# Attention with an off-by-one softmax, then a max-out feed-forward layer: the first two batches in a new order

## The chip, the cores and the metric

The kernel runs on one core of one Trainium2 chip. The metric is device time in microseconds (us) of one execution. Before the change the median of three runs is 368.01 us (367.05 to 368.43). The execution that the profiler recorded took 374.09 us by the same clock, and its span from the first to the last instruction is 372.2 us; all times of single instructions below are from that span.

Five engines work side by side, each on its own list of instructions in order: PE (TensorE, matrix products), DVE (VectorE), ACT (ScalarE), POOL (GpSimd, which here issues the loads) and SP (which here issues stores and crossbar transposes). They wait for one another only through semaphores.

## The reference

```python
# q, k, v: [8 batches, 12 heads, 448 positions, 64], float32
scores = q @ k.T / sqrt(64)
m = max(scores, axis=-1)
e = exp(scores - m)
attn = e / (sum(e, axis=-1) + exp(-m) + 1e-9)        # "softmax off by one"
x = (attn @ v) with the 12 heads side by side        # [3584 tokens, 768]
h = maximum(maximum(x @ w1, x @ w2), x @ w3)         # each w: [768, 768]
out = h @ w_out                                      # [3584, 768] float32
```

Without the maximum, which the kernel leaves out because it cancels, attn = exp(s) / (sum exp(s) + 1).

## The kernel before

The work is cut into 24 **groups**: batch b (8 of them) times g (3), each with four heads. A group needs k and q transposed (head dimension on the partitions), then scores, exponentials, the denominator, and the product with v. Loads by POOL turn float32 into fp16 on the way, except k and q of group 0, which SP and ACT load as float32 into tiles of their own.

**From a loaded tile to the transposed one.** DVE first copies each of k and q so that two heads lie side by side (`copy_qk`); then either PE transposes seven 128x128 blocks for each into PSUM and DVE copies that back (`pe_transpose`), or one crossbar DMA from the SP queue does both (`dma_transpose`). Groups 0 to 6 (`PE_TR = 7`) go over PE, the others over the crossbar.

```python
    def copy_qk(i, n):
        st = state.setdefault(i, {})
        if n == 0:
            st["qk16"] = p16_pool.tile([128, 2, NJ, 2, D], MMDT, tag="qk16", name="qk16")
        src = first["kq"[n]] if i == 0 else raw[i]["kq"[n]]
        nc.vector.tensor_copy(
            out=st["qk16"][:, n], in_=src.rearrange("p s j d -> p j s d")
        )
...
    def pe_transpose(i, n):
        st = state[i]
        if n == 0:
            st["qkT"] = att_pool.tile([128, 2, NJ, 128], MMDT, tag="qkT", name="qkT")
        trT = ps1.tile([128, NJ, 128], MMDT, tag="bank1", name="trT")
        for j in range(NJ):
            nc.tensor.transpose(
                out=trT[:, j, :], in_=st["qk16"][:, n, j].rearrange("p s d -> p (s d)"),
                identity=ident16,
            )
        nc.vector.tensor_copy(
            out=st["qkT"][:, n].rearrange("p j c -> p (j c)"),
            in_=trT.rearrange("p j c -> p (j c)"),
        )
        if n == 1:
            st.pop("qk16")

    def pe_transpose_both(i):
        for n in range(2):
            pe_transpose(i, n)

    def dma_transpose(i):
        st = state[i]
        st["qkT"] = att_pool.tile([128, 2, NJ, 128], MMDT, tag="qkT", name="qkT")
        nc.sync.dma_start_transpose(
            out=st["qkT"].rearrange("p n j c -> p (n j) c"),
            in_=st.pop("qk16").rearrange("p n j s d -> p (n j s d)"),
        )
```

**Scores** fill PSUM tiles of the pool `ps2` (three buffers), and ACT empties them with the exponential. The first batch is cut into two parts of positions (`PARTS`: 192 and 256 columns) so that feed-forward can start before attention of the batch is complete; from group 3 on a group is visited whole, in the units 0 to 2, 3 to 4, and 5 to 6.

```python
    PARTS = ((0, 3), (3, NJ))

    def scores_part(i, part):
        st = state[i]
        q0, q1 = PARTS[part]
        nq = (q1 - q0) * KC
        eT = e_pool.tile([128, NJ, 2, nq], MMDT, tag="eT", name="eTp")
        st["eT", part] = eT
        for j0 in range(0, NJ, 2):
            n = min(2, NJ - j0)
            stp = ps2.tile([128, 2, 512], FP32, tag="bank2", name="stp")
            for jj in range(n):
                score_tile(st["qkT"], stp[:, :, ts(jj, nq)], j0 + jj, q0, q1)
            nc.scalar.activation(
                out=eT[:, j0 : j0 + n].rearrange("p j r q -> p r j q"),
                in_=stp[:, :, 0 : n * nq].rearrange("p r (j q) -> p r j q", j=n),
                func=AF.Exp,
                scale=scale,
                bias=e_b,
            )

    def scores_visit(i, units):
        st = state[i]
        if "eT" not in st:
            st["eT"] = e_pool.tile([128, NJ, 2, S], MMDT, tag="eT", name="eT")
        stps = []
        for j in units:
            stp = ps2.tile([128, 2, 512], FP32, tag="bank2", name="stp")
            score_tile(st["qkT"], stp[:, :, 0:S], j, 0, NJ)
            stps.append((j, stp))
        for j, stp in stps:
            nc.scalar.activation(
                out=st["eT"][:, j], in_=stp[:, :, 0:S], func=AF.Exp, scale=scale, bias=e_b
            )
```

`av_part(i, part)` (letter A below) makes 28 matmuls with ones for the denominator, then on ACT a logarithm (`lnd`) and an exponential (`rb`) for its inverse, 28 matmuls with v, and on DVE the product into `xT`. For whole groups `sum_e`, `den_group` and `av_group` do this.

**Feed-forward** is a queue of `pieces`, each a run of PE matmuls that ends in one DVE operation; `moe(cols)` puts in as many as the credit allows, and after each piece one waiting DVE or SP job from `jobs`. `up_part` pieces are 12 matmuls of 192 or 256 columns (first batch), `up_piece` six of 448, `out_piece` six of 384. The pools `ps1` (two buffers: transposes, numerators, pieces), `ps2` (three), `e` (three) and `ld` (five for q and k, six for v) limit how far one engine runs ahead of another.

**Order of the start and the loop.** A letter is an operation, the digits are group and part (C copies, T transposes on PE, S scores of a part, A attention output of a part, M one piece):

```python
    start = """
        C0 T0 S00 C1 T1 S10 A00
        C2 T2 S20 A10 S01 A20 S11 M1 M1 M1 A01 S21 M1
        C3 M1 T3 M1 A11 M1 M1 A21 M1
    """
```

```python
    for i in range(NG, NI):                       # NG = 3, NI = 24
        ...                                       # loads of group i + 3
        if i == NG:
            gap = sum(w for f, a, w in pieces) / 8

        scores_visit(i, (0, 1, 2))
        if i - 2 >= NG:
            av_group(i - 2)
        scores_visit(i, (3, 4))
        ...                                       # four sum_e jobs
        if on_pe:                                 # i + 1 < PE_TR
            pair_qk(i + 1)
        ...
        moe(gap)
        if on_pe:
            pe_transpose_both(i + 1)
        flush()
        scores_visit(i, (5, 6))
        if i > NG:
            den_group(i - 1)
        if PE_TR <= i + 2 < NI:
            ...                                   # jobs: copy_qk twice, dma_transpose, for i + 2
        ...                                       # two sum_e jobs
        moe(gap)
        flush()
```

Of the kernel before, what the change touches and what calls it, by code (L numbers as in the profile page):

```python
# [16 lines left out]
MMDT = FP16  # L17
# [5 lines left out]
def kernel(  # L23
# [11 lines left out]
    nc = tc.nc  # L35
# [4 lines left out]
    KC = 64  # L40
    NJ = S // KC
# [3 lines left out]
    NG = H // GH  # L45
# [6 lines left out]
            name=nc.get_next_instruction_name(),  # L52
# [10 lines left out]
    e_pool = ctx.enter_context(tc.tile_pool(name="e", bufs=3))  # L63
# [11 lines left out]
    raw = {}  # L75
# [9 lines left out]
    def load_half(eng, dst, name, i, hp):  # L85
        b, g = groups[i]
        src = src_of[name][b].rearrange("(g h) (p j) d -> g p h (j d)", g=NG, j=NJ)[g]
        eng.dma_start(  # L88
            out=dst[hp * KC : hp * KC + KC].rearrange("p s j d -> p s (j d)"),
            in_=src[:, half_heads(name, hp)],  # L90
        )

    def load_group(i, which="qkv"):
        tiles = raw.setdefault(i, {})
        for name in which:
            tiles[name] = ld_pool.tile(
                [128, 2, NJ, D], MMDT, tag="ld_" + name, name="ld_" + name, bufs=6 if name == "v" else 5
            )
            for hp in range(2):
                load_half(nc.gpsimd, tiles[name], name, i, hp)  # L100
# [7 lines left out]
    ident16 = cpool.tile([128, 128], MMDT, name="ident16")  # L108
# [30 lines left out]

    state = {}  # L140
# [4 lines that stand above are left out]
            st["qk16"] = p16_pool.tile([128, 2, NJ, 2, D], MMDT, tag="qk16", name="qk16")  # L145
        src = first["kq"[n]] if i == 0 else raw[i]["kq"[n]]
        nc.vector.tensor_copy(  # L147
            out=st["qk16"][:, n], in_=src.rearrange("p s j d -> p j s d")
        )

    def pair_qk(i):
        for n in range(2):
            copy_qk(i, n)

    def pe_transpose(i, n):
        st = state[i]
        if n == 0:
            st["qkT"] = att_pool.tile([128, 2, NJ, 128], MMDT, tag="qkT", name="qkT")
        trT = ps1.tile([128, NJ, 128], MMDT, tag="bank1", name="trT")
        for j in range(NJ):  # L160
            nc.tensor.transpose(  # L161
                out=trT[:, j, :], in_=st["qk16"][:, n, j].rearrange("p s d -> p (s d)"),
                identity=ident16,
            )
# [4 lines left out]
        if n == 1:  # L169
            st.pop("qk16")  # L170

    def pe_transpose_both(i):
        for n in range(2):
            pe_transpose(i, n)
# [17 lines left out]
    def score_tile(qkT, out, j, q0, q1):  # L192
        for r, c in TILES:
            h = half(QK_HALF[r, c])
            nc.tensor.matmul(  # L195
                out=out[half(c), r],
                lhsT=qkT[half(r), 0, j, h],
                rhs=qkT[half(r), 1, q0:q1, h],
                start=True,
                stop=True,  # L200
# [42 lines left out]
    def den_group(i):  # L243
        st = state[i]
        dps = ps2.tile([128, 2, 512], FP32, tag="bank2", name="den")
        av_tiles(
            [dps[:, r, 0:S] for r in range(2)],
            lambda r, c: ones16[half(r)],
            lambda r, c: st["eS"][half(r), c],
            True,  # L250
            True,
        )
        lnd = small.tile([128, 2, S], FP32, tag="lnd", name="lnd")
        nc.scalar.activation(out=lnd, in_=dps[:, :, 0:S], func=AF.Ln, bias=one_b)  # L254
        st["rb"] = small.tile([128, 2, S], FP32, tag="rb", name="rb")
        nc.scalar.activation(out=st["rb"], in_=lnd, func=AF.Exp, bias=ln_lam, scale=-1.0)  # L256
# [21 lines left out]

    PARTS = ((0, 3), (3, NJ))

    def scores_part(i, part):
        st = state[i]
        q0, q1 = PARTS[part]
        nq = (q1 - q0) * KC
        eT = e_pool.tile([128, NJ, 2, nq], MMDT, tag="eT", name="eTp")
        st["eT", part] = eT
        for j0 in range(0, NJ, 2):
            n = min(2, NJ - j0)
            stp = ps2.tile([128, 2, 512], FP32, tag="bank2", name="stp")
            for jj in range(n):  # L290
# [124 lines left out]
    pieces = []  # L415
# [13 lines left out]
    jobs = []  # L429
# [18 lines left out]
    NI = len(groups)  # L448
    PE_TR = 7

    load_weight(0)
    load_weight(1)
# [1 line left out]
    load_weight(2)  # L454
    load_group(4, "kq")
    load_group(3, "v")

    def add_parts(b, i, part):
        for fp in range(NFC // 2):
            pieces.append((up_part, (b, fp, i, part), 1.0))  # L460

    for i, part in ((0, 0), (1, 0), (2, 0), (0, 1), (1, 1), (2, 1)):
        add_parts(0, i, part)
    ops = {
        "C": pair_qk,
        "T": pe_transpose_both,
        "S": scores_part,
        "A": av_part,
        "M": moe,
    }  # L470
# [12 lines left out]
    ]  # L483
    add_out(0)

    for i in range(NG, NI):
        b, g = groups[i]
        if i == 3:
            load_group(5, "kq")
            load_group(4, "v")  # L490
            load_weight(3)
            load_group(5, "v")
            load_group(6)
        elif i + 3 < NI:
# [5 lines left out]
        scores_visit(i, (0, 1, 2))  # L500
        if i - 2 >= NG:
            av_group(i - 2)
        scores_visit(i, (3, 4))
        for j in (1, 2, 3, 4):
            jobs.append((sum_e, (i, j)))
# [9 lines left out]
        scores_visit(i, (5, 6))  # L515
        if i > NG:
            den_group(i - 1)
        if PE_TR <= i + 2 < NI:
            jobs.append((copy_qk, (i + 2, 0)))
            jobs.append((copy_qk, (i + 2, 1)))  # L520
            jobs.append((dma_transpose, (i + 2,)))
        for j in (5, 6):
            jobs.append((sum_e, (i, j)))
        moe(gap)
        flush()
    av_group(NI - 2)
# [37 lines left out]
```

## Time and profile before

| What | Value |
|---|---|
| median time | 368.01 us |
| span of the profiled execution | 372.2 us |
| PE busy | 329.0 us (88%), 3170 matmuls |
| DVE busy | 248.8 us (67%) |
| ACT busy | 206.2 us (55%) |
| POOL busy | 91.9 us (25%) |
| crossbar transposes, us from issue to landing | 17 of them: 3.9 least, 4.3 median, 11.8 most |
| moved by DMA | 41.02 MB |

The share of busy time is an average over stages that are limited by different things. The row of 40 slices on the profile page (each 9.3 us) shows the stages; the table of windows gives busy time of each engine between two times; the list of waits says for whom an engine sat idle; the chain follows the work that ended last back to the start. Matmuls are pipelined, so a busy PE isn't PE at its peak.

### The profile page before, as it was taken

The numbers are of one execution on the slowest core, as the hardware profiler recorded it, in microseconds if no ns is written. First come the engines' busy times: TensorE is split into PE (matmuls) and PEld (weight loads), VectorE is DVE, ScalarE is ACT, GpSimd is POOL, SyncE is SP. The second block draws the span as 40 slices with busy tenths as digits, with TensorE's granted clock in tenths as the row PEclk, the third lists the DMA queues.
The fourth block names the chain that finished last, engine by engine and source line by source line (L and its number), as shares of the span: only waits on it lengthen the run. The fifth ranks groups of instructions, "written<-read, shape, count | busy, mean of one in ns | idle before, by whom it ended". The sixth has DMA issues, their size and how long they took to land.

```text
span 372.2 us, 7685 instructions
## 1 busy us (share of the span) xinstructions
PE 329.0 (88%) x3170; PEld 185.7 (50%) x3170; DVE 248.8 (67%) x446; ACT 206.2 (55%) x226; POOL 91.9 (25%) x158
## 2 busy tenths in 40 slices
PE   0667877889399999999999999999999999998994
PEld 0555765654144455445544554455454555444552
DVE  0531445788647887878788888878788786754552
ACT  1459725688556658565846766586566668420000
POOL 7835864032130332033213303321100000000000
PEclk9999999999889999999999999999999999999999
DMA  8999999025983587767868488848622360013006
GB/s 162 197 206 205 181 184 148 2 34 98 153 154 64 77 126 178 148 90 106 161 112 125 79 191 150 110 74 159 112 51 50 86 136 0 2 42 86 1 2 169
DMA packets 59524, 41.02 MB, mean 110 GB/s; under 512 B 34400, under 2 KB 55904, under 8 KB 59488
## 3 DMA queue, kind: packets, MB, share of 16 engines
q0 software_dynamic: 23424, 20.78, 38.3%
q1 hardware_dynamic: 35776, 19.27, 23.9%
q10 hardware_dynamic: 288, 0.46, 0.6%
q8 instruction: 25, 0.41, 0.5%
q14 instruction: 11, 0.09, 0.1%
HBM read 42.47 MB, written 11.01 MB: 144 GB/s over the span
## 4 chain that ended last, share of the span: by engine, by line
PE 77%; ACT 8%; DVE 6%; DMA 5%; issue 2%; SPq 0%; DVEq 0%
PE p_i L351 40%; PE op_ps L394 13%; PE av L235 7%; PE stp L195 7%; PE p_i L372 5%; DVE xT L274 3%; DMA qkT<-qk 3%; ACT eTp L292 3%; ACT eT L213 3%; PE den L235 2%; DMA first_k<-in_k_dram 2%; PE trT L161 2%; ACT rb L323 1%; ACT lnd L319 1%; DVE qk L147 1%
## 5 line engine op out<-in xcount | busy, mean ns | idle before, releaser
L213 ACT ACTIVATE eT<-stp,e_b 128x896 f16<-128x896 f32 x147 | 136.7, 1009 | 90.8 <-PE stp L195 90.8
L351 PE MATMUL p_i<-xT,w 128*128 128x448 f16 x756 | 148.1, 352 | 3.5 <-DVE xT L274 1.6
L351 PEld LDWEIGHTS <-w 128*128 128x128 f16 x756 | 72.8, 98 | 75.1 <-issue 10.1
L361 DVE TENSOR_TENSOR hT<-hT,p_i 128x448 f16<-128x448 f16 x84 | 52.2, 621 | 27.5 <-PE p_i L351 27.5
L195 PE MATMUL stp<-qkT 64*64 64x448 f16 (+2 forms) x756 | 54.9, 356 | 16.3 <-DMA qkT<-qk 5.6
L88 POOL DMA_DIRECT2D ld_v<-in_v_dram x48 | 28.8, 611 | 153.9 <-PE stp L195 121.9
L221 DVE TENSOR_TENSOR eS<-eS,eT 128x896 f16<-128x896 f16 x105 | 65.0, 619 | 2.4
L394 PE MATMUL op_ps<-w,hT 128*128 128x384 f16 x336 | 57.8, 327 | 0.0
L195 PEld LDWEIGHTS <-qkT 64*64 64x64 f16 x756 | 22.8, 114 | 43.3 <-issue 32.7
L394 PEld LDWEIGHTS <-hT 128*128 128x128 f16 x336 | 31.5, 98 | 24.9 <-issue 2.8
L401 DVE TENSOR_SCALAR o_sb<-op_ps 128x384 f32<-128x384 f32 x56 | 31.0, 554 | 13.8 <-PE op_ps L394 13.7
L235 PE MATMUL av<-eT,ld_v 64*64 64x448 f16 x588 | 36.9, 362 | 0.8 <-DVE hT L359 0.4
L359 DVE CAST hT<-p_i 128x448 f16<-128x448 f32 x42 | 26.2, 625 | 15.0 <-PE p_i L351 15.0
L274 DVE TENSOR_TENSOR xT<-av,rb 128x448 f16<-128x448 f32 x42 | 24.3, 620 | 15.7 <-PE av L235 15.7
L235 PEld LDWEIGHTS <-ld_v 64*64 64x64 f16 x756 | 26.7, 114 | 12.7 <-issue 7.7
L88 POOL DMA_DIRECT2D ld_k<-in_k_dram x46 | 28.4, 637 | 5.4 <-DMA w<-in_moe_w_dram 2.6
L88 POOL DMA_DIRECT2D ld_q<-in_q_dram x46 | 27.9, 624 | 6.4 <-DMA w<-in_moe_w_dram 2.8
L292 ACT ACTIVATE eTp<-stp,e_b 128x768 f16<-128x768 f32 (+3 forms) x24 | 19.9, 912 | 17.1 <-PE stp L195 17.1
L254 ACT ACTIVATE lnd<-den,one_b 128x896 f32<-128x896 f32 x21 | 21.2, 1009 | 8.8 <-PE den L235 8.8
L372 PE MATMUL p_i<-xT,w 128*128 128x192 f16 (+1 forms) x216 | 22.4, 259 | 2.5 <-DVE xT L335 2.5
L256 ACT ACTIVATE rb<-lnd,ln_lam 128x896 f32<-128x896 f32 x21 | 21.9, 1042 | 0.7
L372 PEld LDWEIGHTS <-w 128*128 128x128 f16 x216 | 19.1, 98 | 5.6 <-issue 4.2
(32 smaller groups left out, 130.7 us busy)
## 6 DMA issues: line engine op xcount, KB each, us to landing
out_dram<-o_sb SPq DMA_DIRECT2D x56, 192.0 KB, 3.1
ld_v<-in_v_dram POOLq DMA_DIRECT2D x48, 112.0 KB, 4.0
ld_k<-in_k_dram POOLq DMA_DIRECT2D x46, 112.0 KB, 4.4
ld_q<-in_q_dram POOLq DMA_DIRECT2D x46, 112.0 KB, 4.2
w<-in_moe_w_dram POOLq DMA_DIRECT2D x3, 576.0 KB, 11.2
w<-in_moe_w_dram POOLq DMA_DIRECT2D x6, 288.0 KB, 9.2
w<-in_moe_w_out_dram POOLq DMA_DIRECT2D x3, 384.0 KB, 7.9
first_k<-in_k_dram SPq DMA_DIRECT2D x2, 224.0 KB, 6.2
```

The costliest lines, as they stand in the source:

```text
L88: eng.dma_start(out=dst[hp * KC : hp * KC + KC].rearrange("p s j d -> p s (j d)"), in_=src[:, half_heads(name, hp)],)
L195: nc.tensor.matmul(out=out[half(c), r], lhsT=qkT[half(r), 0, j, h], rhs=qkT[half(r), 1, q0:q1, h], start=True, stop=True,)
L213: nc.scalar.activation(out=st["eT"][:, j], in_=stp[:, :, 0:S], func=AF.Exp, scale=scale, bias=e_b)
L221: nc.vector.tensor_tensor(out=st["eS"], in0=st["eT"][:, 0] if j == 1 else st["eS"], in1=st["eT"][:, j], op=ALU.add,)
L235: nc.tensor.matmul(out=outs[r][half(c)], lhsT=weights(r, c), rhs=moving(r, c), start=start, stop=stop,)
L274: nc.vector.tensor_tensor(out=xT[b][:, 2 * g + r, :], in0=banks[r][:, 0:S], in1=st["rb"][:, r], op=ALU.mult)
L292: nc.scalar.activation(out=eT[:, j0 : j0 + n].rearrange("p j r q -> p r j q"), in_=stp[:, :, 0 : n * nq].rearrange("p r (j q) -> p r j q", ...
L351: nc.tensor.matmul(out=p_i[:, 0:S], lhsT=w_sb[i][:, dc, ts(fc, 128)], rhs=xT[b][:, dc, :], start=(dc == 0), stop=(dc == NDC - 1),)
L361: nc.vector.tensor_tensor(out=dst, in0=dst, in1=p_i[:, 0:S], op=ALU.max)
L372: nc.tensor.matmul(out=p_i[:, ts(j, nq)], lhsT=w_sb[i][:, dc, ts(2 * fp + j, 128)], rhs=xT[b][:, dc, q0 * KC : q1 * KC], start=(dc == 0), ...
L394: nc.tensor.matmul(out=op_ps[:, 0:NW], lhsT=hT[bp][:, fc, ts(t, 128)], rhs=wout_sb[:, fc, ts(nh, NW)], start=(fc == 0), stop=(fc == NFC - 1),)
L401: nc.vector.tensor_scalar(out=o_sb[:, ts(nh, NW)], in0=op_ps[:, 0:NW], scalar1=1.0 / LAMBDA, scalar2=None, op0=ALU.mult,)
```

## The change

It changes the order of the first two batches (groups 0 to 5) and the way to their transposed k and q. The aim is to keep PE supplied in the stretch ahead of the steady loop.

- **Groups 1 to 4 are transposed on PE straight from the loaded tile.** The pairing copy on DVE is gone for them. A transpose now takes one head pair's half, 128 partitions by 64 columns, into the upper or lower 64 partitions of the PSUM tile: 14 transposes for each of k and q instead of seven.
- **The crossbar serves from group 5 on** (`PE_TR = 5`), not from group 7.
- **The pairing copy** that is left (group 0, and groups 5 to 23) walks its source in order and scatters its output, where it walked its output in order.
- **Scores of a part are in two calls** (`S`: units 0 to 5; `s`: unit 6), so that other PE work stands between them.
- **The scores of group 3** (`U3`, `V3`, `W3`) stand amid the feed-forward pieces of the start; the loop begins at group 4. Its gaps are a sixth of the pieces that are left, not an eighth, and group 4 has a third, smaller gap.
- The loads of groups 4 to 6 and of `w_out` stand ahead of the start in the program; POOL's own list of loads has the same order as before.

```diff
-            out=st["qk16"][:, n], in_=src.rearrange("p s j d -> p j s d")
+            out=st["qk16"][:, n].rearrange("p j s d -> p s j d"), in_=src
...
         for j in range(NJ):
-            nc.tensor.transpose(
-                out=trT[:, j, :], in_=st["qk16"][:, n, j].rearrange("p s d -> p (s d)"),
-                identity=ident16,
-            )
+            if i == 0:
+                nc.tensor.transpose(
+                    out=trT[:, j, :], in_=st["qk16"][:, n, j].rearrange("p s d -> p (s d)"),
+                    identity=ident16,
+                )
+                continue
+            for s in range(2):
+                nc.tensor.transpose(
+                    out=trT[s * KC : s * KC + KC, j, :], in_=raw[i]["kq"[n]][:, s, j], identity=ident16
+                )
...
-    def scores_part(i, part):
+    def scores_part(i, part, last=False):
...
-        for j0 in range(0, NJ, 2):
+        for j0 in (6,) if last else (0, 2, 4):
...
-    PE_TR = 7
+    PE_TR = 5
...
     start = """
-        C0 T0 S00 C1 T1 S10 A00
-        C2 T2 S20 A10 S01 A20 S11 M1 M1 M1 A01 S21 M1
-        C3 M1 T3 M1 A11 M1 M1 A21 M1
+        C0 T0 S00 T1 s00 S10 T2 s10 A00 S20 A10 s20 S01 A20 s01
+        S11 M1 s11 M1 M1 A01 S21 M1 s21 M1 T3 M1 A11 U3 M1 A21 V3 T4 E30 M1 M1 W3 E31 X5 F
     """
...
-    for i in range(NG, NI):
+    for i in range(NG + 1, NI):
...
-        if i == NG:
-            gap = sum(w for f, a, w in pieces) / 8
+        if i == NG + 1:
+            gap = sum(w for f, a, w in pieces) / 6
...
         if i - 2 >= NG:
             av_group(i - 2)
-        scores_visit(i, (3, 4))
...
-        if on_pe:
-            pair_qk(i + 1)
+        else:
+            moe(gap / 3)
+        visit_b(i)
+        sums(i, 0)
```

In the new start U, V and W are the three visits to a whole group's scores, E its `sum_e` jobs, X the jobs for a crossbar transpose (two copies and the DMA), and F carries out all waiting jobs.

More of the change, by code (lines that the diff above doesn't have):

```diff
@@ L155, in pe_transpose @@
     def pe_transpose(i, n):
-        st = state[i]
+        st = state.setdefault(i, {})
         if n == 0:
@@ L168, in pe_transpose @@
         )
-        if n == 1:
-            st.pop("qk16")
     def pe_transpose_both(i):
@@ L284, in scores_part @@
         nq = (q1 - q0) * KC
-        eT = e_pool.tile([128, NJ, 2, nq], MMDT, tag="eT", name="eTp")
-        st["eT", part] = eT
-        for j0 in range(0, NJ, 2):
+        if not last:
+            st["eT", part] = e_pool.tile([128, NJ, 2, nq], MMDT, tag="eT", name="eTp")
+        eT = st["eT", part]
+        for j0 in (6,) if last else (0, 2, 4):
             n = min(2, NJ - j0)
@@ L456 @@
     load_group(3, "v")
+    load_group(5, "kq")
+    load_group(4, "v")
+    load_weight(3)
+    load_group(5, "v")
+    load_group(6)
     def add_parts(b, i, part):
@@ L463, with visit_a, visit_b, visit_c @@
         add_parts(0, i, part)
+    def visit_a(i):
+        scores_visit(i, (0, 1, 2))
+    def visit_b(i):
+        scores_visit(i, (3, 4))
+    def visit_c(i):
+        scores_visit(i, (5, 6))
+    def sums(i, n):
+        for j in (1, 2, 3, 4) if n == 0 else (5, 6):
+            jobs.append((sum_e, (i, j)))
+    def transpose_later(i):
+        jobs.append((copy_qk, (i, 0)))
+        jobs.append((copy_qk, (i, 1)))
+        jobs.append((dma_transpose, (i,)))
     ops = {
+        "X": transpose_later,
+        "F": flush,
         "C": pair_qk,
@@ L467 @@
         "S": scores_part,
+        "s": lambda i, part: scores_part(i, part, True),
         "A": av_part,
         "M": moe,
+        "U": visit_a,
+        "V": visit_b,
+        "W": visit_c,
+        "E": sums,
     }
     start = """
-        C0 T0 S00 C1 T1 S10 A00
-        C2 T2 S20 A10 S01 A20 S11 M1 M1 M1 A01 S21 M1
-        C3 M1 T3 M1 A11 M1 M1 A21 M1
+        C0 T0 S00 T1 s00 S10 T2 s10 A00 S20 A10 s20 S01 A20 s01
+        S11 M1 s11 M1 M1 A01 S21 M1 s21 M1 T3 M1 A11 U3 M1 A21 V3 T4 E30 M1 M1 W3 E31 X5 F
     """
@@ L484 @@
     add_out(0)
-    for i in range(NG, NI):
+    for i in range(NG + 1, NI):
         b, g = groups[i]
[L488 to L494, printed above, removed]
+        if i + 3 < NI:
             load_group(i + 3)
         on_pe = i + 1 < PE_TR
-        if i == NG:
-            gap = sum(w for f, a, w in pieces) / 8
-        scores_visit(i, (0, 1, 2))
+        if i == NG + 1:
+            gap = sum(w for f, a, w in pieces) / 6
+        visit_a(i)
         if i - 2 >= NG:
             av_group(i - 2)
-        scores_visit(i, (3, 4))
-        for j in (1, 2, 3, 4):
-            jobs.append((sum_e, (i, j)))
-        if on_pe:
-            pair_qk(i + 1)
+        else:
+            moe(gap / 3)
+        visit_b(i)
+        sums(i, 0)
         if i - 2 >= NG and g == 1:
@@ L514 @@
         flush()
-        scores_visit(i, (5, 6))
-        if i > NG:
-            den_group(i - 1)
+        visit_c(i)
+        den_group(i - 1)
         if PE_TR <= i + 2 < NI:
[L519 to L523, printed above, removed]
+            transpose_later(i + 2)
+        sums(i, 1)
         moe(gap)
```

## The prediction

> **What bounds the kernel now.** I read the 40 slices first. The PE row is full from the twelfth slice on and far from it before; DMA is at nine tenths until the seventh slice, then nearly empty.
>
> ```profile
> PE   0667877889399999999999999999999999998994
> ...
> DMA  8999999025983587767868488848622360013006
> ```
>
> So the steady loop is bound by PE, and all there is to win lies in the first 102 us. The table of windows, asked at the borders of the start, puts a size on it (columns: window, its length, then busy us and instructions of PE, PEld, DVE, ACT, POOL, granted clock, DMA share, GB/s).
>
> ```profile
> 10.00:57.80 47.80, 35.22 (x672) 29.85 (x673) 17.61 (x36) 27.46 (x36) 30.80 (x52) 1.00 1.18 194
> 57.80:65.10 7.30, 5.66 (x67) 3.93 (x67) 4.62 (x9) 4.72 (x6) 2.74 (x5) 1.00 0.99 141
> 65.10:102.10 37.00, 27.53 (x304) 17.50 (x300) 29.02 (x52) 26.91 (x29) 7.14 (x12) 0.96 0.53 69
> 102.10:105.90 3.80, 3.78 (x44) 1.87 (x48) 0.00 (x0) 2.80 (x3) 0.00 (x0) 0.50 0.95 255
> ```
>
> PE idles 12.6 us up to 57.8, 1.6 us up to 65.1, 9.5 us up to 102.1; no other engine is near full in these windows, so it is the order of work that costs. The last row shows a clock of 0.50 for 3.8 us. The waits of PE from 58 to 102.2 us say what the largest gap was for:
>
> ```profile
> PE stp L195 <- DMA qkT<-qk: 5.6, 1, 5.6
> PE stp L195 <- ACT eT L213: 3.8, 7, 0.7
> ```
>
> The chain of work shows that wait as one transfer, and the scores behind it:
>
> ```profile
> 90.24 11.83 DMA qkT<-qk
> 102.12 1.33 PE stp L195 x12
> ```
>
> It is the first crossbar transpose (group 7). It took 11.83 us against a median of 4.3; it was issued only 5.9 us before PE ran dry, and the timeline shows six loads issued between 90.78 and 94.4 and six stores around it.
>
> In the first 30 us the chain goes DVE copy, PE transpose, DVE copy, scores, ACT, one after the other; two of its links:
>
> ```profile
> 22.59 0.54 DVE qk L147
> 23.18 1.69 PE trT L161 x14
> ```
>
> **What the Trainium skill says.** "TensorE: Matmul & The Clock Gate", Part 1: PE starts at half rate, rises after some 3.4 us of sustained work and falls back after an idle window of that length. The trace agrees: 14 transposes take 1.69 us at 23 us and seven take 0.55 at 47 us, and the half clock sits around the 5.6 us wait. "VectorE: DVE Perf Modes", What auto-detection actually checks: a copy within SBUF gains a second read port if the outermost dimensions of both sides are even. The outer dimension of the pairing copy was 7 and becomes 2; its row now shows 610 ns for fp16 and 1086 for float32. "TensorEngine Tiling (Array Packing)", Overview: tiles of half the columns can run side by side; no transpose of this shape is in the trace. "DMA: Bandwidth & Descriptors", Queues, rings and completion order: an engine takes queues in turn, packet by packet. The 11.83 us beside loads agree.
>
> **The change, part by part.** I follow the letters of the new start with durations of the trace.
>
> *First copies.* 896 elements took 1086 ns; with two per cycle of 0.96 GHz 896/2/0.96 = 467 ns go away, so about 0.62 us (an estimate from that page). The two copies stand ahead of 14 transposes (1.92 us, cold) that PE then binds: scores of group 0 begin at 12.3, not 12.76. **Gain 0.5.**
>
> *Transposes without pairing.* Per group 1 to 4 two copies of 0.61 leave DVE; PE has 28 half-width transposes for 14. If two run side by side a group takes the 1.68 us of now (cold), else 3.36. From 12.3: S00 1.17, T1 1.68 to 3.36, s00 0.2, wait for the last PSUM copy 0.65, S10 1.17, T2 1.68 to 3.36, s10 0.2, A00 1.34 + 1.38, and 0.58 until the first exponential of S20: 22.4 to 25.7. I take **24**; it now is at 26.16. **Gain 2.2 in all here**, the 0.5 included. The worst case wins nearly nothing, because s10 then stands behind T2 and ACT waits.
>
> *From there to the end of group 3's scores.* ACT leads at first: S20 three at 0.91, ln and exp of A10 1.2, s20 0.59, S01 3.0, A20 1.2, s01 0.69, together 9.4: at 33.4. Then PE leads. A piece is 1.05 (36 matmuls, 3.14), A of part 1 1.9, S of part 1 0.82, s 0.14, a whole visit 0.69 + 0.46 + 0.46, T 1.1 to 2.2 warm, say 1.65. Last unit of S11 to T3: 0.14 + 1.05 + 0.14 + 2.1 + 1.9 + 0.82 + 1.05 + 0.14 + 1.05 + 1.65 = 10.0; M to T4: 1.05 + 1.9 + 0.69 + 1.05 + 1.9 + 0.46 + 1.65 = 8.7; M1 M1 W3: 2.6. That is 21.3, with 1 us for waits W3 ends at **55.7** (53 to 58.5). Now the same work ends at 65.1 less two second-part pieces already done by then (2.8): 62.3. **Gain 6.6.**
>
> *Groups 4 to 6.* A gap is now a sixth of nine pieces of 1.395 and six of 1.0, so group 4 takes six pieces (8.4 us) with its scores and denominator 2.0: 10.4. Groups 5 and 6 have some 8.4 of PE work, and ACT needs seven exponentials of 1.007 and two of 1.03: 9.1 each. From 55.7 group 7 begins at 84.3, 28.6 later. Now the same stretch takes 102.1 - 62.3 = 39.8. **Gain 11.2**: 5.6 is the transposes' wait, 2.2 the PE transposes of groups 5 and 6 (four times 0.55), the rest waits for ACT and one visit less that runs thin.
>
> *Clock.* Without that wait the 3.8 us at half clock go: **1.9.**
>
> *Crossbar of group 5.* Its copies stand behind the last sum of group 3, so at 55.7 + 1.5 (exponentials) + 0.7 (sum) + 0.8 (two copies, an estimate as above) it is issued at about 59; PE needs it at 55.7 + 10.4 = 66.1. At the median of 4.3 it is early by 3. At 11.8 it is late by 5. Loads of groups 8 and 9 still run at 59 to 63, so I put **1 us lost**.
>
> *Steady loop.* Its PE list is the same from group 7 on. The faster copies (610 to about 380 ns, estimated likewise) free DVE, which at 67% doesn't bind. Nothing.
>
> Span: 372.2 - 6.6 - 11.2 - 1.9 + 1 = 353.5; by 368.01/372.2 that is 349.5 us of device time.
>
> One doubt pushes it up. The profiled execution took 374.09 us, 6 more than the timed median, about as much as the transpose's wait and the half clock together (5.6 + 1.9). If timed executions do not meet that wait, 7.5 us are not there to win: 368 - 6.6 - 11.2 - 1.9 + 7.5 + 1 = 356.8. I give that 4 in 10: 0.6 x 349.5 + 0.4 x 356.8 = **352.4, say 352**.
>
> **Rivals.** (1) *The wait moves to group 5*: the crossbar now starts while the load queue is still full (its share is 0.99 even at 57.8 to 65.1), against a lead of 7 us. For it: the 11.83. Against: by 63 loads should have drained. It would give back 5 us and 2 of clock: 357 to 360. (2) *Half-width transposes run one by one*, or their weight loads do: 3.4 us a group cold, 2.2 warm. T1 to T4 then take 5.6 us more than side by side, 2.8 more than I put in: 355. (3) *DMA binds the start*: w3, and k and q of group 4, must be there sooner. The third up weight was issued until 27.3 and landed in 9 to 11 us, by 38; its first piece comes at about 47. k and q of group 4 were issued by 30.5 and took 8.2: 39, needed at 51. So this is hidden by 9 us or more; if it did bind, the start would end near the old 62 and the change be worth 9 to 13 us, 355 to 359. (4) *ACT binds*: from 24 to 33 and in groups 5 and 6 it does, and is in the sum. If it waited for PE at each letter as now, 3 us more. (5) *PE warms sooner* because it idles less before 30 us: up to 3 us less, 349.
>
> **Range.** The rivals reach down to 345 (no doubt about the profile, warm early) and up to 360 (the wait moved). Slower than now would need a new wait of 16 us, and none is in sight; within 2% means above 360.65, which rivals 1 and 2 together would reach. So 352, range 345 to 360; faster by over 2% 0.90, within 2% 0.09, slower 0.01.
>
> **What would show it.** Scores of group 0 near 12.3 and the first exponential of S20 near 24; the half-width transposes' own row, 14 in about 0.6 us warm if side by side, 1.1 if not; W3 ending near 55.7; group 7's scores near 84 to 85; PE busy about 327; no wait of PE for the crossbar above 2 us and no half clock after the start; the pairing copy near 380 ns. I am wrong if PE waits for the crossbar at group 5, if transposes take above 3 us a group warm, or if the loop from group 7 on takes longer than the 268 us it takes now (372.2 - 102.1 less 1.9).

## The result and the profile after

| What | Before | After |
|---|---|---|
| median time | 367.92 us (367.05 to 368.43, four runs) | 355.25 us (353.24 to 359.33, four runs) |
| span of the profiled execution | 372.2 us | 357.6 us |
| PE busy | 329.0 us | 324.9 us |
| first exponential of group 2, part 0 | 26.16 us | 20.94 us |
| scores of group 7 begin | 102.1 us | 88.89 us |
| from there to the end | 270.1 us | 268.7 us |

The ratio is 0.964, with an interval of 0.957 to 0.971. The changed kernel run once more beside the first experiments gave 358.87 us and 0.974 (0.968 to 0.980). Single executions of it spread over 6 us, and their granted clock goes along: 353.24 us at 1.000, 353.86 at 0.999, 356.63 at 0.994, 359.33 at 0.986. The last is the profiled one, so the profile below may show something that the others met only in part or not at all.

The rows of the 40 slices on the page of the changed kernel (each 8.9 us):

```profile
PE   0779879499999999999999999999999999898994
...
PEclk9998999789999999999999999999999999999999
DMA  8999999978965797688965895587312540022006
```

PE now is full from the ninth slice on (71.5 us); before it was so from the twelfth (102.4 us). One deep hole is left, the eighth slice. The clock dips there and in the ninth, and once before, in the fourth.

The table of windows has the same columns as before the change (window, length, busy us of PE, PEld, DVE, ACT and POOL with instructions, clock, DMA share, GB/s). Its borders are the end of group 3's scores, the first scores of group 5, and those of group 7:

```profile
10.00:52.20 42.20, 35.45 (x769) 30.05 (x767) 15.70 (x33) 31.85 (x42) 24.64 (x41) 0.96 1.16 191
52.20:68.97 16.77, 10.47 (x108) 7.45 (x100) 11.71 (x22) 10.13 (x11) 9.10 (x16) 0.95 1.30 154
68.97:88.89 19.92, 19.45 (x192) 10.97 (x192) 13.25 (x25) 15.36 (x17) 7.13 (x12) 0.87 0.85 124
```

PE idles 6.8 us in the first, 6.3 in the second and 0.5 in the third. The third runs at a clock of 0.87: PE works there all the time, but not at full rate. The 0.96 of the first is a half clock from 26.4 to 29.8 us, well ahead of the hole. (The column has no record before 19.6 us and shows 1.00 there, though the durations below are those of half rate.) The waits of PE between 10 and 105 us (waits, count, longest) name the hole:

```profile
PE stp L198 <- DMA qkT<-qk: 5.1, 1, 5.1
PE stp L198 <- ACT eT L216: 2.3, 5, 0.7
```

and the chain of work shows the transfer and what it released:

```profile
56.48 12.45 DMA qkT<-qk
68.97 1.33 PE stp L198 x12
```

It is the crossbar transpose of group 5, now the first. It was issued at 56.48, 7.4 us ahead of PE's need (63.9), and took 12.45 us. So the wait that stood ahead of group 7 stands ahead of group 5: it wasn't removed, it moved on with the transfer that comes first.

The transposes straight from the loaded tile, in the timeline of PE (start, us, what; "x14" is seven blocks in two halves):

```profile
13.13 0.96 PE L168 MATMUL trT<-ident,ld_k 128*64 128x128 f16 x14
13.88 0.96 PE L168 MATMUL trT<-ident,ld_q 128*64 128x128 f16 x14
...
38.90 0.58 PE L168 MATMUL trT<-ident,ld_k 128*64 128x128 f16 x14
39.61 0.58 PE L168 MATMUL trT<-ident,ld_q 128*64 128x128 f16 x14
```

Warm, 14 halves take 0.58 us, what seven whole ones took before (chain of work):

```profile
47.08 0.55 PE trT L161 x7
```

So the two halves run side by side. And the copies, in the groups of the page (count, busy us, mean ns, idle before):

```profile
L147 DVE COPY qk<-ld_k 128x896 f16<-128x896 f16 x19 | 7.3, 385 | 0.0
L147 DVE CAST qk<-first_k 128x896 f16<-128x896 f32 x1 | 0.6, 628 | 8.0 <-DMA first_k<-in_k_dram 8.0
```

385 and 628 ns stand where 610 and 1086 stood. The first exponentials of group 2 in the timelines of ACT, before and after:

```profile
26.16 2.96 ACT L292 ACTIVATE eTp<-stp,e_b 128x768 f16<-128x768 f32 x4 [4.22 <-PE stp L195]
```

```profile
20.94 2.46 ACT L296 ACTIVATE eTp<-stp,e_b 128x768 f16<-128x768 f32 x3
```

ACT had stood idle for 4.22 us; now it goes on without a pause.

### The profile page after: what moved, and what is told of

Read it like the earlier page. It is cut to its first block, busy times and chain, and to the rows that moved or that the text cites. A ratio compares the mean times of both kernels' runs of the same rounds, so it can differ in the third digit from the quotient of the medians.

```text
span 357.6 us, 7731 instructions
## 1 busy us (share of the span) xinstructions
PE 324.9 (91%) x3198; PEld 182.8 (51%) x3198; DVE 234.5 (66%) x434; ACT 205.7 (58%) x226; POOL 92.2 (26%) x158
## 4 chain that ended last, share of the span: by engine, by line
PE 79%; ACT 7%; DMA 6%; DVE 5%; issue 2%; SPq 0%; DVEq 0%
PE p_i L355 41%; PE op_ps L398 15%; PE stp L198 8%; PE av L238 8%; PE p_i L376 4%; DMA qkT<-qk 3%; DVE xT L277 3%; ACT eT L216 3%; DMA first_k<-in_k_dram 2%; PE den L238 2%; ACT eTp L296 2%; PE trT L168 1%; ACT rb L327 1%; ACT lnd L323 1%; DVE qkT L171 1%
## 5 line engine op out<-in xcount | busy, mean ns | idle before, releaser
L198 PEld LDWEIGHTS <-qkT 64*64 64x64 f16 x756 | 22.0, 112 | 35.5 <-issue 27.1
```

The source lines that it names most:

```text
L198: nc.tensor.matmul(out=out[half(c), r], lhsT=qkT[half(r), 0, j, h], rhs=qkT[half(r), 1, q0:q1, h], start=True, stop=True,)
```

## The experiments

Two questions were open: what made the first crossbar transpose slow, and which part of the change carries the gain. Ratios are to the kernel before on the same chip, with a 95% interval; they leave out executions more than 1.5% above the fastest of their kernel.

### The changed kernel again

No edit: the code as changed.

> The changed kernel again, unaltered, to see how far its wait for the crossbar of group 5 differs between executions. If the wait is the source of its spread (353.2 to 359.3 us so far), the executions with a granted clock of 1.00 are the short ones (353 to 354) and those with 0.99 or less the long ones (356 to 359). If the spread has another source, clock and time do not go together.

358.87 us (355.49 to 359.99), ratio 0.974 (0.968 to 0.980). The profile repeats the first: the crossbar of group 5 was issued at 57.19 and took 12.28 us, PE waited 4.9 us, and half clock followed from 69.08 to 72.49. Clock and time go together only loosely, though: executions of 355.49 and 358.17 us both had 0.993. The mean clock also holds losses that have nothing to do with this wait, such as a half clock from 28.12 to 31.53 us in this profile, so it doesn't show where an execution lost its time.

### The first crossbar issued eleven microseconds sooner

```diff
-        ... T3 M1 A11 U3 M1 A21 V3 T4 E30 M1 M1 W3 E31 X5 F
+        ... T3 M1 A11 U3 M1 X5 F A21 V3 T4 E30 M1 M1 W3 E31 F
```

> The two copies and the crossbar of group 5 are issued one attention output earlier, at about 47.5 us and not 56.5. Theory (the transfer takes some 12 us beside the loads and needs that much lead): it lands at about 60, PE does not wait for it at 63.9, no half clock at 67 to 74, span 357.6 - 5.1 - 3.4 = 349, executions within 1 us of each other at 350 to 352. Rival (DVE would wait for the loads of group 5, or the transfer is served only after the loads are done, at 65 or later): the wait stays at 3 us or more, or moves to DVE before A21, and the time does not fall.

353.6 us (351.24 to 358.62), ratio 0.961 (0.955 to 0.967). In the profiled execution, the fastest, the transfer was issued at 45.72, took even longer (16.4 us), and landed at 62.08, 0.8 us before PE used it; no half clock follows, and the span is 349.5 us. So enough lead hides the transfer. But the executions spread as widely as before; what the one of 358.62 us met was not profiled.

### No crossbar before group 7

Groups 5 and 6 go over PE, too, straight from the loaded tile.

```diff
-    PE_TR = 5
+    PE_TR = 7
-        ... M1 M1 W3 E31 X5 F
+        ... M1 M1 W3 E31 F
```

> The crossbar starts at group 7 as in the kernel before; groups 5 and 6 are transposed on PE from the loaded tiles. Theory (the wait for the early crossbar costs 5.1 us and 3.4 of half clock, the PE transposes it saves only 4 x 0.58 = 2.3): no wait of PE above 1 us, span about 351.5, a little longer than with the earlier crossbar. Rival (the first crossbar transpose is slow wherever it stands): PE waits for group 7 as in the kernel before, 4 to 6 us, and the time is 355 to 358.

354.51 us (354.25 to 356.08), ratio 0.966 (0.964 to 0.969), and no wait of PE for a transfer among the largest of its list:

```profile
PE stp L198 <- ACT eT L216: 2.5, 5, 0.7
PE den L238 <- ACT eTp L296: 1.8, 3, 1.1
```

Its first crossbar was issued at 75.74 and took 4.0 us, after the loads of the start had thinned out. That the crossbar serves from group 5 on gains nothing that shows: its PE work saved, 2.2 us by the prediction, is given back by the wait. The spread goes with it: 1.8 us from best to worst here, 4.5 in the changed kernel on the same chip.

### One v buffer less

If loads that run far ahead slow the crossbar, fewer buffers should hold some of them back.

```diff
-   ... tag="ld_" + name, name="ld_" + name, bufs=6 if name == "v" else 5
+   ... tag="ld_" + name, name="ld_" + name, bufs=5
```

> Five buffers for v, not six, and nothing else: the loads of v of group 8 and of q and k of group 9 (0.7 MB) wait until attention of group 3 is done, so fewer loads are in the rings beside the crossbar of group 5. Theory (it takes 12 us because it takes turns with loads): issued at 56.5 it lands in 5 to 9 us, PE waits 0 to 2 us, span 350 to 353. Rival (the first crossbar takes 12 us in any case): it lands after 11 to 12 us again and PE waits 4 to 5 us.

355.23 us (352.17 to 358.91), ratio 0.964 (0.959 to 0.969). The transfer hardly changed, as the chain shows:

```profile
56.85 11.89 DMA qkT<-qk
```

PE waited 4.6 us. Packets of loads still moved beside it until about 65 us, so the edit hadn't taken them away. It left open whether the first crossbar is slow by itself.

### Loads held until the crossbar of group 6 has landed

POOL issues the loads from its own list in order. A copy of one column of group 6's transposed tile, ahead of the loads of group 7, makes that list wait for the transfer.

```diff
+    fence = cpool.tile([128, 1], MMDT, name="fence")
...
-        if i + 3 < NI:
+        if i > NG + 1 and i + 3 < NI:
             load_group(i + 3)
...
+        if i == NG + 1:
+            nc.gpsimd.tensor_copy(out=fence, in_=state[6]["qkT"][:, 1, NJ - 1, 0:1])
+            load_group(i + 3)
```

> POOL copies one column of group 6's transposed tile before it issues the loads of group 7, so no load is issued between those of group 6 and the landing of the crossbar of group 6; nothing else changes. Theory (the crossbar takes 12 us only because loads share the DMA engines with it): the crossbar of group 5 is issued near 56.5 as before and lands in 4 to 5 us, PE does not wait for it, no half clock after 30 us, span 349 to 350, executions at 351 to 352 and close together. Rival (the first crossbar transpose of a program is slow by itself, as the run with five v buffers would also allow): it takes 9 to 12 us again and PE waits 2 to 5 us. A second rival: the loads of groups 7 to 9, held back some 14 us, come too late and PE waits for those.

The crossbar of group 5, issued at 55.30, took 4.0 us, and PE didn't wait for it. The chain shows the one of group 6 as fast, and then the next:

```profile
62.49 3.97 DMA qkT<-qk
...
73.75 27.81 DMA qkT<-qk x2
```

That settles the cause: the same transfer in the same place takes 4.0 us without loads (in two more kernels further below, too) and 12 with them. But the total is 356.24 us (354.51 to 357.14), ratio 0.964 (0.959 to 0.969), no better than after. The held loads ran beside the crossbar of group 7, which took 11.9 us, and PE waited there:

```profile
PE stp L200 <- DMA qkT<-qk: 4.3, 1, 4.3
```

Half clock followed from 85.76 to 89.17. The wait moved on once more.

### Pairing copies and whole transposes in the new order

Groups 1 to 4 get their pairing copy back (C1 to C4) and are transposed whole.

```diff
-            if i == 0:
+            if True:
...
-        C0 T0 S00 T1 s00 S10 T2 s10 A00 ...
-        ... s21 M1 T3 M1 A11 U3 M1 A21 V3 T4 ...
+        C0 T0 S00 C1 T1 s00 S10 C2 T2 s10 A00 ...
+        ... s21 C3 M1 T3 M1 A11 U3 M1 A21 C4 V3 T4 ...
```

> Groups 1 to 4 get the pairing copies and the 14 wide transposes back; order and crossbar as in the changed kernel. Theory of the prediction (the copies lie on the chain, direct transposes win 2 us): the first exponential of the scores of group 2 comes at 22 to 23 us, not 20.9. Rival (with scores of the group before standing ahead of each transpose the two copies of 0.38 us are hidden, and two half-width transposes side by side cost PE what one wide one does): it comes within 0.4 us of 20.9, and the span up to the crossbar's issue is unchanged. The total time can differ by 3 us either way through the wait for the crossbar, so it is not what decides.

The first exponential of group 2 starts at 20.74 us, against 20.94 after the change; counted from the first scores of group 0, as k and q of group 0 land earlier or later from one execution to the next, that is 9.03 us against 8.91. So the copies lie beside other work. PE still ran at half rate for most of this stretch, as the denominators and numerators of group 0 show (timeline of PE):

```profile
18.08 1.33 PE L238 MATMUL den<-eTp,ones 64*64 64x192 f16 x28
19.20 1.32 PE L238 MATMUL num<-eTp,ld_v 64*64 64x192 f16 x28
20.32 0.70 PE L198 MATMUL stp<-qkT 64*64 64x192 f16 x24
```

One transpose waited for its copy, that of group 4 (in brackets what it waited for):

```profile
48.68 0.95 PE L162 MATMUL trT<-ident,qk 128*128 128x128 f16 x14 [1.50 <-DVE qk L147]
```

The total, 360.24 us (355.45 to 360.91), ratio 0.971 (0.962 to 0.979), has in it a crossbar of 13.84 us and a wait of 6.5, so it doesn't tell the parts apart. The experiment without an early crossbar further below does.

### The old direction of the pairing copy

```diff
-            out=st["qk16"][:, n].rearrange("p j s d -> p s j d"), in_=src
+            out=st["qk16"][:, n], in_=src.rearrange("p s j d -> p j s d")
```

> The pairing copy walks its output in order again. Expected: 1080 ns for the float32 copies and 610 for the fp16 ones, not 630 and 380; scores of group 0 begin 0.4 to 0.5 us later, at 12.5; the crossbar of group 5 is issued 0.5 us later and PE waits for it as much longer; from group 7 on nothing. In all 0.5 to 1 us. If DVE were near its limit in the loop, several us.

The copies took 610 and 1086 ns again. Scores of group 0 began at 12.24 us instead of 12.03, but the loads had landed half a microsecond earlier in this execution. From the start of the first copy to these scores it is 3.78 us against 3.07 (3.78 in the kernel before, too): the old direction costs the start 0.7 us. From the first exponential of group 7 to the end both take 267.2 us, so in the loop it costs nothing. The total, 360.36 us (355.09 to 360.47), ratio 0.971 (0.962 to 0.979), can't be read for this, as the wait for the crossbar scatters by more than the copies are worth (its transfer took 10.24 us here, and PE waited 3.3).

### Direct transposes alone, in the order of before

The kernel before, with groups 1 to 6 transposed straight from the loaded tile and C1 to C3 gone.

```diff
-            nc.tensor.transpose(
-                out=trT[:, j, :], in_=st["qk16"][:, n, j].rearrange("p s d -> p (s d)"), ...
+            for s in range(2):                      # i > 0
+                nc.tensor.transpose(
+                    out=trT[s * KC : s * KC + KC, j, :], in_=raw[i]["kq"[n]][:, s, j], ...
...
-        C0 T0 S00 C1 T1 S10 A00
-        C2 T2 S20 A10 ...
+        C0 T0 S00 T1 S10 A00
+        T2 S20 A10 ...
...
-        if on_pe:
-            pair_qk(i + 1)
```

> The kernel before with one part of the change: groups 1 to 6 are transposed on PE straight from the loaded tile, no pairing copies for them; order and crossbar (from group 7) as before. Theory (in the old order the copies of group 2 stand behind the product of group 0 on DVE, and PE idles 1.4 us for them): PE reaches the transposes of group 2 at 21.8, not 23.18, and the kernel is 1.4 to 2 us faster, 365.5 to 366. Rival (what waits there is ACT's work, not the copy): under 0.5 us.

366.39 us (365.21 to 367.47), ratio 0.993 (0.990 to 0.996). The transposes of group 2 start at 22.42 us, not 23.18, and are held by the copy into `xT`, no longer by their own:

```profile
22.42 0.96 PE L168 MATMUL trT<-ident,ld_k 128*64 128x128 f16 x14 [0.60 <-DVE xT L339]
```

The first exponential of group 2 comes at 25.04 us (26.16 before). Its span in the profile is 364.8 us with a wait for the crossbar of 1.9 us, where the profile of before shows 5.6 us. The gain is small but clear of noise, and larger than the 1.1 us of the start: the fastest of 18 executions is 1.4 us below the fastest of 25 of before (365.21 against 366.66), the median 2.7 us below theirs (369.11). None is above 367.47, where those of before reach 372.53. Whether the edit also shortens the wait for the crossbar isn't settled by one profile of each.

### Two holds, for groups 6 and 7

```diff
-        if i + 3 < NI:
+        if i > NG + 2 and i + 3 < NI:
             load_group(i + 3)
...
+        if i < NG + 3:
+            nc.gpsimd.tensor_copy(out=fence, in_=state[i + 2]["qkT"][:, 1, NJ - 1, 0:1])
+        if i == NG + 1:
+            load_group(7)
+            load_group(8, "qk")
+        if i == NG + 2:
+            load_group(8, "v")
```

> As the run with one hold of POOL, with two: loads of group 7 and of q and k of group 8 go out when the crossbar of group 6 has landed, v of group 8 and what follows when that of group 7 has. Theory (loads and crossbar slow each other down only when in flight together, and three times 4 us of pause cost the loads nothing that is needed): the crossbars of groups 5, 6 and 7 take 4 to 5 us each, PE waits for none of them, no half clock after 30 us, span 349 to 350, executions at 351 to 352.5 and within 1.5 us of each other. Rival (the wait moves on to the next crossbar once more, or DVE waits for q and k of group 8): a wait of 2 to 5 us at group 7 or 8, 354 to 356.

357.97 us (354.47 to 360.33), ratio 0.967 (0.962 to 0.972). The crossbars of groups 5, 6 and 7 took 4.0, 3.9 and 4.9 us. The one of group 8 met the loads (chain, then the waits of PE):

```profile
84.97 16.49 DMA qkT<-qk
```

```profile
PE stp L200 <- DMA qkT<-qk: 3.5, 1, 3.5
```

So holding loads back a few times only chooses which transfer meets the heap of them.

### Group 3's scores back in the loop

The kernel with no crossbar before group 7, with group 3 visited in the loop as before the change and the gaps an eighth.

```diff
-        ... T3 M1 A11 U3 M1 A21 V3 T4 E30 M1 M1 W3 E31 F
+        ... T3 M1 A11 M1 M1 A21 M1
-    for i in range(NG + 1, NI):
+    for i in range(NG, NI):
-        if i == NG + 1:
-            gap = sum(w for f, a, w in pieces) / 6
+        if i == NG:
+            gap = sum(w for f, a, w in pieces) / 8
...
-        else:
-            moe(gap / 3)
```

> As the run with the crossbar from group 7 (354.5 us, steady), but the scores of group 3 are visited in the loop again, with gaps of an eighth, as in the kernel before. Theory (one visit that ACT paces at 9.1 us and that is filled too thinly goes away when group 3's scores stand amid the feed-forward of the start): 3 to 5 us longer, 357.5 to 359.5. Rival (the earlier and split scores of groups 0 to 2 make the gain): under 1 us longer.

359.43 us (358.80 to 360.02), ratio 0.973 (0.968 to 0.978); the kernel without this edit had 354.51 and 0.966, on another chip. No large wait for a transfer (1.0 us in all). What is there instead is PE standing behind ACT and DVE:

```profile
PE stp L198 <- ACT eT L216: 3.9, 8, 0.7
PE p_i L376 <- DVE xT L339: 2.5, 2, 1.2
```

### The new order alone

Pairing copies and whole transposes for all groups up to 6, no early crossbar; left of the change are the order, the split scores and the direction of the copy.

```diff
     # on top of "pairing copies and whole transposes in the new order"
-    PE_TR = 5
+    PE_TR = 7
-        ... E30 M1 M1 W3 E31 X5 F
+        ... E30 M1 M1 W3 E31 F
+        if on_pe:
+            pair_qk(i + 1)
```

> The new order of the start alone: pairing copies and wide transposes on PE for groups 1 to 6, crossbar from group 7 as before. Against the run with direct transposes and the crossbar from group 7 (354.5 us). Theory (direct transposes win little once other PE work stands ahead of each; only group 4's wait of 1.5 us for its copy and 2 x 0.38 us of DVE a group are left): 355 to 356.5. Rival (direct transposes carry 2 us or more of the gain): 357 or longer.

355.68 us (355.52 to 357.04), ratio 0.963 (0.959 to 0.967). That is the whole ratio of the change. On the same chip, the kernel with group 3 back in the loop is 3.75 us slower (359.43 less 355.68), although it has the direct transposes, which this one lacks. The scores of group 7 begin, in the timelines of this kernel and of that one:

```profile
85.16 0.92 PE L198 MATMUL stp<-qkT 64*64 64x448 f16 x12
```

```profile
89.04 0.76 PE L198 MATMUL stp<-qkT 64*64 64x448 f16 x12 [0.96 <-DMA qkT<-qk]
```

That is 3.9 us, of which 0.96 is the wait in brackets, for the first crossbar of that kernel; the spans of the two executions are 3.1 us apart. Group 3's place is not the whole gain of the order: with group 3 back in the loop, 10.3 us of median are still won (359.43 against 369.75). Direct transposes on top of the new order bring little: 355.68 against 354.51 us, on two chips, with ratios of 0.963 and 0.966 whose intervals overlap.

### A hold at every group

One copy by POOL per group from 4 to 20, each behind a landed crossbar, each followed by one group's worth of loads, so that no heap can form.

```diff
-        if i + 3 < NI:
-            load_group(i + 3)
...
+        if i + 3 < NI:
+            nc.gpsimd.tensor_copy(out=fence, in_=state[i + 2]["qkT"][:, 1, NJ - 1, 0:1])
+            load_group(i + 3, "qkv" if i == NG + 1 else "v")
+            if i + 4 < NI:
+                load_group(i + 4, "qk")
```

> After the landing of every crossbar (groups 6 to 22), and not before, POOL issues one group's worth of loads: v of the next group, q and k of the one after it (behind the first also q, k and v of group 7). So every crossbar has the DMA engines to itself but for stores, and no backlog of loads is left to be made up. Theory (with two holds the wait had only moved to the crossbar of group 8, which met the loads held back): all crossbars up to group 9 take 4 to 6 us, PE waits for none of them above 1 us, span 349 to 351, executions at 351 to 353. Rival (the order of stores and crossbars on the SP queue, or loads that now come too late, makes the wait): PE still waits 2 us or more for a crossbar, or DVE for q or k, and the time is 354 or more.

352.98 us (352.49 to 354.18, six runs), ratio 0.957 (0.953 to 0.961). PE waits for no transfer; the largest waits between 10 and 150 us are

```profile
PE stp L200 <- ACT eT L218: 2.0, 4, 0.7
PE av L240 <- DVE o_sb L407: 1.9, 2, 1.2
```

The first crossbars took 4.0, 3.9, 5.9, 8.7, 8.4 and 6.0 us: not all are fast, but none is late. It is the steadiest of the kernels with an early crossbar, 1.7 us from best to worst against 6.1 after the change, and the lowest median. It was not run on the same chip as the changed kernel; of that kernel's two intervals one (from 0.957) overlaps with its own (to 0.961), the other doesn't.

## Why the prediction was right

352 us was predicted, with a range of 345 to 360; 355.25 was measured. The order of work wins, as predicted. That the number fits so well is in part luck: in the profiled span the start was put 3.6 us too long, the stretch from there to group 7 was put 7.15 us too short, and most executions, before and after, seem to meet less of their wait than the profiled ones. Point by point:

- *First copies*: 0.62 us predicted, 0.63 measured; scores of group 0 at 12.03 us (12.3 predicted). Right; the run that put the old copies back shows that they cost the start 0.7 us, a little more than the 0.5 that was put in.
- *Transposes without pairing*: the first exponential of group 2 was put at 24 and came at 20.94, below the best case of 22.4. Side by side was right. That the missing copies shorten this stretch was not: from the first scores of group 0 to this exponential it is 8.91 us after the change, 9.03 with pairing copies in the new order, and 13.40 before. The order does it. Direct transposes alone, in the old order, moved the exponential by 1.1 us. What was mis-sized is the sum, 10.05 us in the best case: it put whole durations one behind the other, though PE begins the next group of matmuls before the last one's recorded end. Denominators and numerators were put at 1.34 and 1.38 us; in the lines of the kernel with pairing copies, at half rate as the best case had it, each takes 1.12 from start to start. The clock comes on top, as rival 5 had it (full rate from 19.6 us, before from 30.8): the eight executions of the new start that had full rate by 17.9 us took 7.9 to 8.2 us for the stretch, the four that had it only after 19.5 us took 8.9 to 9.2.
- *To the end of group 3's scores*: 55.7 predicted, 52.1 measured. From the exponential on it is 31.2 us against 31.7 predicted; the 3.6 us are the head start.
- *Group 4*: 10.4 us predicted; PE wanted group 5 at 63.9, so 11.8. 1.4 us too little.
- *Crossbar of group 5*: this is the step that failed. "1 us lost" was put in; the profiled execution lost 5.05 us, and 1.7 us more at half clock in groups 5 and 6 (19.92 us where 18.2 was predicted). Rival 1 came true there, and with it a sign of being wrong that the prediction had named. The estimate rested on loads being drained by 63 us. When the transfer was issued, some 200 packets of loads moved per us, and when most of it was through, at 66 us, they were back at 220.
- *Group 7*: 84.3 plus the 1 us was predicted, 88.89 measured. The terms above add up: -3.6 + 1.4 + 4.05 + 1.7 = 3.55.
- *Steady loop*: 268 us predicted from group 7 on, 268.7 measured. The faster copies change nothing there, as predicted (267.2 us from its first exponential with either copy).
- *From span to time*: the sum was multiplied by 368.01/372.2, as if every execution were as far below its profile as that median. The doubt was probably the right reading: beside the first experiments six of seven executions of before lie within 366.29 to 367.64 us and one at 372.7, so most seem not to pay the wait that its profile shows, and of the 7.5 us most weren't there to win. This is argued from times alone; only an execution of 374.09 us was profiled. (On the other three chips before spreads more evenly, from 367 to 373 us.) With 356.8 for that case, less 3.6 for the start, plus 1.4 for group 4, less the 1 us for executions that lose nothing to the crossbar, the same sum gives 353.6; the execution at clock 1.000 took 353.24, and holding the loads at every group gives 352.98 as a rule.

So the gain that timed executions see is the order of the start with the faster first copies (and of it, group 3's scores amid feed-forward, with the gaps that go with them, 3 to 4 us). In that order direct transposes add no more than about 1 us, and the early crossbar nothing, unless the loads are kept off it. That the changed kernel's executions between 353 and 359 us differ by this wait is likely, from the steadiness of the four kernels that have no such wait (1.2 to 1.8 us from best to worst); it isn't shown, as only executions at the slow end of that scatter were profiled.

## What to carry to other kernels

Where engines wait for one another in a chain, first move other work between the links; removing a link pays only if it still is on the path afterwards, as the pairing copies here were not: in the old order the kernel without them was 1.4 to 2.7 us faster, in the new one about 1 at most. Before a transfer is issued sooner, look at what the queues carry at the new time: its best duration is worth nothing if it lands among loads. Where a profiled execution is slower than the timed median, ask which of its waits the others meet before counting that wait as a gain.

## What was not expected of the hardware

A crossbar transpose within SBUF and loads under way slow each other, and together they move less than an even share would give. Packets in a window, by queue kind (packets, MB, share of 16 engines): the changed kernel from 61 to 64 us, with both under way, then from 66 to 68, with hardly anything but loads (36 packets of the crossbar's queue are in the same view):

```profile
q1 hardware_dynamic: 1248, 0.32, 106.8%
q0 software_dynamic: 93, 0.07, 22.9%
```

```profile
q0 software_dynamic: 449, 0.36, 116.1%
```

and the kernel with the loads held, from 57 to 59 us, with the crossbar alone:

```profile
q1 hardware_dynamic: 1482, 0.37, 99.1%
```

Alone the crossbar moves 741 packets per us in that window; beside loads it is 416, and the loads fall from 225 to 31. As shares of what each does alone these are 0.56 and 0.14, together 0.70. The whole transfer has 1824 packets. With the loads held they all moved within the 4 us. In the changed kernel two had moved 2.5 us after its issue, 1617 by 64 us, and the last tenth took until 68.93, when the loads were back at 220 per us. In its second run there even were two microseconds, 66 to 68, with 81 packets of loads and 23 of the crossbar in all.

The prediction had cited the Trainium skill, "DMA: Bandwidth & Descriptors", Queues, rings and completion order, that an engine takes its queues in turn, packet by packet. These counts can't say whether it does so here. On that page a packet bundles several descriptors, while what the profile counts is 256 bytes for the crossbar and some 800 for a load (0.32 MB in 1248, 0.36 MB in 449); 13 of one to one of the other may be turns or not. Why the two together reach only 0.70 is left open.

A wait of about 5 us costs more than itself: half clock followed from 67.37 to 74.2 us in the changed kernel, and from 85.76 to 89.17 after the 4.3 us where the wait had moved to group 7. After the waits of 3.3 us (old direction of the copy) and 3.5 us (two holds) none followed. That agrees with the Trainium skill, "TensorE: Matmul & The Clock Gate", Part 1, which has the clock fall back to half after an idle window of some 3.4 us.

The clock also fell without such a wait. In the changed kernel it was half from 26.41 to 29.83 us, and the longest pause of PE in the seven microseconds before is 1.05 us, all pauses together 2.55. Numerators of two groups, the first ahead of it, the second in it (timeline of PE):

```profile
22.45 0.77 PE L238 MATMUL num<-eTp,ld_v 64*64 64x192 f16 x28
26.82 1.40 PE L238 MATMUL num<-eTp,ld_v 64*64 64x192 f16 x28
```

In six of the other thirteen profiles PE ran 3.4 us at half clock in the same way before 32 us; that of the kernel with a hold at every group shows full rate from 20.64 us to 351.7. What decides it isn't shown. A stretch of which nearly half is transposes did raise the clock: PE was at full rate from 19.6 us, after 7.5 us of transposes and scores in which no pause is above 0.41 us.
